# Attention with two feed-forward blocks on one Trainium2 core: how the last six result banks are evicted and stored

## The chip, the cores and the metric

The kernel runs on one NeuronCore of a Trainium2 chip. The metric is the device time of one execution in microseconds (us). The kernel before took 1049.45 us as the median of three runs (1048.07 to 1259.41).

## The reference

Everything is float32. Four batches of 576 rows and eight heads go through a thresholded softmax attention, and the result, as 2304 tokens of 512 numbers, through two feed-forward blocks:

```python
scores = scale * np.matmul(q, k.transpose(0, 1, 3, 2))
thresh = np.max(scores, axis=-1, keepdims=True) - tau
scores = np.where(scores >= thresh, scores, -1000000000.0)
...
h = x @ w_in
g = np.maximum(h, 0.0) + alpha * np.minimum(h, 0.0)
x = g @ w_out
...
a = x @ w1
b = x @ w2
h = a * b @ w3
return h @ w_out
```

The output is one array of 2304 rows of 512 float32 numbers (2 KB a row), batch after batch: rows 576 t to 576 t + 575 belong to batch t.

## The kernel before, in words

The kernel has three stages: attention, the first feed-forward block, and the second one. The change touches only how the second block's results leave the core.

**The second block.** w3 @ w_out is multiplied out beforehand (the tiles `wp`). The 2304 tokens are then taken in three passes (`NPASS`, L1181) of 768 tokens each, two halves of 384. In a pass the loop of L1381 goes over eight slices `f` of the hidden width. For each slice TensorE multiplies the moving tiles `T` by the stationary tiles `sw` in seven products (`product`, L1336, matmuls at L1341), ScalarE and VectorE put these together (`copy_of`, `tt`) and split the product into pairs `x`, and TensorE adds `x` times `wp` to six accumulating PSUM banks, `accs[0]` to `accs[5]` (`d_piece`, L1354, matmuls at L985). Four of these banks carry the name `acc`, two the name `h`. In the last slice of a pass each bank is finished by three matmuls, in the order 3, 4, 5, 0, 1, 2 (L1448).

**Evicting and storing.** When a bank is finished, `ev` (L1466) copies it to an SBUF tile `o` of 128 x 512, and `store` (L1469) sends that tile, 256 KB, to the output in DRAM from SyncE's queue. `GROUPS` (L1199) says which rows a bank holds. In passes 0 and 1, and in four banks of pass 2, these are 128 rows of one batch (every fourth of its first 512), which L1472 writes as 128 rows. Banks 4 and 5 of the last pass hold the last 64 rows of two batches each; L1475 addresses them as an array of 2 x 64 x 512, one transfer for both batches. So in the last pass the stores are, in order: one of 128 rows (bank 3), two of 2 x 64 rows (banks 4 and 5), and three of 128 rows (banks 0, 1, 2).

**What sets the order.** Each operation is given to a planner (`list_order`, L34) with the engines that may do it and an assumed cost. `{"A": 0.48, "V": 0.6}` at L1478 means ScalarE (A) or VectorE (V), whichever the planner finds earlier; "S" is SyncE, "T" TensorE, "D" a mark without an instruction. The planner's result is the order of the instructions on every engine; on the chip each engine then runs its own list in order and waits on semaphores where data is not there yet. In the kernel before the planner gave all eighteen evictions of L1467 to ScalarE.

After the last store, SyncE waits until all stores have landed (these waits have the line of the launch, L1517), and a few closing semaphores and drains end the program.

Of the kernel before, what the change touches and what calls it, by code (L numbers as in the profile page):

```python
# [120 lines left out]
def kernel(  # L121
# [25 lines left out]
    nc = tc.nc  # L147
    B, H, S, D = q.shape
# [8 lines left out]
    SM = 512  # L157
    ST = S - SM
# [62 lines left out]
    with tc.manual_schedule():  # L221
# [118 lines left out]
        for h in range(2):  # L340
# [4 lines left out]
            out=kscale, in0=tau_sb, scalar1=0.0, scalar2=1.0 / float(D) ** 0.5, op0=ALU.is_ge, op1=ALU.mult  # L345
# [223 lines left out]
        def op(key, P, engine, emit, deps=(), take=None, free=()):  # L569
            at = AT[key + "_0" if not P and key + "_0" in AT else key]  # L570
            ops.append(Op({engine: 0.0}, emit, PER * P + at, deps, take, free))
            named[key, P] = ops[-1]
            return ops[-1]
# [7 lines left out]
        for P in range(NPAIR):  # L581
            for n in "qk":
                ld = op("a" + n, P, "S", lambda e, P=P, n=n: load_pair(P, n), spl.get((P - 2, n), ()))
                spl[P, n] = []
                on = "P" if P else "V"
# [18 lines left out]
            for what in ("q", "tails", "k"):  # L604
# [7 lines left out]
                    take="ptp" if what == "tails" else "s",  # L612
# [3 lines left out]
                if what != "q":  # L616
# [7 lines left out]
                    free=[t],  # L624
# [4 lines left out]
            for what in ("q", "tails") if not P else ():  # L629
# [6 lines left out]
                    take="s" if what == "q" else "ptp",  # L636
# [7 lines left out]
                    free=[t],  # L644
# [5 lines left out]
            for j in range(9):  # L650
                u = 9 * P + j
                c, h = j // 2, j % 2
# [6 lines left out]
                    take="s",  # L659
# [11 lines left out]
                    take="praw" if j == 8 else "p" if h == 0 else None,  # L671
                    free=[Q, E],
# [12 lines left out]
                for g, src in groups:  # L685
# [7 lines left out]
                        take="ptp",  # L693
                        free=ms[:1],
# [7 lines left out]
                        take="pt" if new else None,  # L702
                        free=[T],
# [4 lines left out]
                if j in (3, 8):  # L708
                    half = int(j == 8)
                    V = op(  # L710
                        f"V{half}",
                        P,
                        "T",
                        lambda e, P=P, half=half: pv(P, half),
                        evd + [lv],
                        take="ptp",
                        free=[first],
                    )
# [8 lines left out]
                        free=[V],  # L727
# [3 lines left out]
        for f in range(NW):  # L731
            ld = op("w0", f, "S", lambda e, f=f: load_w_in(f), [w_done[f - 1]] if f else [])
            c = op("w1", f, "A", lambda e, f=f: low_w_in(f), [ld])
            m = [ld]
            for i in range(4):
# [6 lines left out]
                    take="m" if i == 0 else None,  # L742
# [4 lines left out]
            hi = op("w7", f, "A", lambda e, f=f: hi_w_in(e, f), [a])  # L747
# [289 lines left out]
        for t in order:  # L1037
# [4 lines left out]
            for f in range(NF):  # L1042
# [6 lines left out]
                    take="h",  # L1049
                    free=[hl[0] for hl in xl],  # L1050
# [20 lines left out]
                g = op({"V": part(n, 0.61)}, prelu, now + 3.5, [u], free=[hj])  # L1071
                h, l = split(n, lambda gt=gt, n=n: gt()[:, 0:n], gs, now + 4.3, [g], "gs", free=[u])

                def x2_job(e, f=f, n=n, acc=acc, gs=gs):
# [17 lines left out]
                    take="acc" if f == 0 else None,  # L1092
                    free=[h],
# [43 lines left out]
        for i in range(NF2):  # L1137
# [20 lines left out]
            for part_ in range(2):  # L1158
# [5 lines left out]
                    take=None if part_ else "h",  # L1164
                    free=[w3_ops[part_].slot],
# [15 lines left out]
        NPASS = B * S // (2 * HT)  # L1181
# [199 lines left out]
        for i, (p, f) in enumerate(order2):  # L1381
            if i + 2 < len(order2):
                S_of[i + 2], S_made[i + 2] = stationary(order2[i + 2][1], now + FP - 3)
            end = i == len(order2) - 1
            T_next = None
            if f == NF2 - 1 and p + 1 < NPASS:
                T_next = moving(p + 1, now + 1.0, None)
            s, m = S_of.pop(i), T_of
            made = S_made.pop(i)
            t = {n: temp() for n in ("u", "v", "c11", "c12")}  # L1390

            def J(k, bank_, first, deps, prio, s=s, m=m):
                o = pe(
                    6 * MH, lambda e: product(bank_, s[k], m[k], first), prio,
                    deps + [o for o in s[k][1]] + [m[k][1], m[k][2]],
                )
                if f == NF2 - 1:
                    o.free.append(m[k][1])
                    m[k][1].left += 1
                return o  # L1400

            def tt(dst, x, y, how, cost, prio, deps, take=None, free=(), engines=None):
                return op(
                    engines or {"V": cost},
                    lambda e: ENG[e].tensor_tensor(out=dst(), in0=x(), in1=y(), op=how),  # L1405
                    prio, deps, take=take, free=free,
                )

            def copy_of(dst, src, prio, deps):
                return op({"A": part(HT, 0.62)}, lambda e: nc.scalar.copy(out=dst(), in_=src()), prio, deps, take="ct")  # L1410

            bx, by = (x_bank, y_bank) if i % 2 == 0 else (y_bank, x_bank)
            X, Y = (lambda b=bx: b()[:, 0:HT]), (lambda b=by: b()[:, 0:HT])
            P_ = 0.56
            q = now
            j1 = J(1, bx, True, x_free, q)
            c1 = copy_of(t["u"], X, q + 1.3, [j1])
            j6 = J(6, by, True, y_free, q + 1.04)
            u2 = tt(t["u"], Y, t["u"], ALU.add, P_, q + 2.3, [j6, c1])
            d_next(q + 2.1, 2)  # L1420
            j2 = J(2, bx, False, [c1], q + 3.5)
            c11 = copy_of(t["c11"], X, q + 4.6, [j2])
            j5 = J(5, by, True, [u2], q + 4.5)
            v5 = tt(t["v"], Y, t["u"], ALU.add, P_, q + 5.8, [j5, u2], take="ct")
            d_next(q + 5.5, 2)
            j7 = J(7, bx, True, [c11], q + 6.9)
            c22 = tt(t["v"], X, t["v"], ALU.add, P_, q + 8.0, [j7, v5])
            j3 = J(3, by, False, [v5], q + 8.0)
            c12 = tt(t["c12"], Y, t["u"], ALU.add, P_, q + 9.1, [j3, u2], take="ct")
            d_next(q + 9.0, 1 if not end else 0)  # L1430
            j4 = J(4, bx, False, [c22], q + 9.7)
            c21 = tt(t["u"], X, t["u"], ALU.add, P_, q + 10.8, [j4, c12])
            d_next(q + 10.7, 1 if not end else 99)
            x_free, y_free = [c12], [c21]
            for h, l in made:
                h.left += 1
            j2.free.append(made[0][0])
            j5.free.append(made[1][0])
            j4.free.append(made[3][0])
            j3.free.append(made[2][0])  # L1440
            ab1 = tt(t["c12"], t["c12"], t["v"], ALU.mult, 0.56, q + 9.7, [c12, c22], free=[v5])
            ab0 = tt(t["u"], t["c11"], t["u"], ALU.mult, 0.56, q + 11.4, [c21, c11], free=[c11])
            gs = [None, None]
            for half, src, made_, frees, at in ((1, "c12", ab1, c12, 10.3), (0, "u", ab0, c1, 12.0)):
                g_ = part_pair("x", bufs=4)
                h, l = split(HT, t[src], g_, q + at, [made_], "x", free=[frees], costs=(0.66, 0.73))
                gs[half] = (g_, h, l)
            for g in (3, 4, 5, 0, 1, 2):  # L1448
                half = g // 3

                def go(prio, g=g, half=half, gs=gs, p=p, f=f):
                    last = f == NF2 - 1
                    _, h, l = gs[half]
                    o = pe(
                        3 * MF, d_piece(g, gs, f, f == 0, last), prio,
                        [h, l, wp_ops[f]] + (evicted[g] if f == 0 else []),
                    )
                    if g % 3 == 2:
                        o.free.append(h)
                        h.left += 1  # L1460
                    if not last:
                        return
                    on = ("u", "gs", "m")[g % 3] if p == NPASS - 1 else ("u", "gs")[g % 2]
                    out_ = lazily(lambda: dn.tile([128, 512], F32, tag=on, name="o", bufs=3 if on == "m" else 2))

                    def ev(e):  # L1466
                        (nc.scalar.copy if e == "A" else nc.vector.tensor_copy)(out=out_(), in_=accs[g]())  # L1467

                    def store(e):  # L1469
                        t_, c = GROUPS[p][g]  # L1470
                        if t_ < B:
                            dst = out[t_ * S : t_ * S + SM, :].rearrange("(p c) d -> p c d", c=4)  # L1472
                            nc.sync.dma_start(out=dst[:, c, :], in_=out_())
                        else:
                            dst = out.rearrange("(b s) d -> b s d", b=B)[2 * c : 2 * c + 2, SM:S, :]  # L1475
                            nc.sync.dma_start(out=dst, in_=out_())

                    v = op({"A": 0.48, "V": 0.6}, ev, prio + 0.7, [o], take=on)  # L1478
                    evicted[g] = [v]
                    s_ = op({"S": 0.65}, store, prio + 1.2, [v])  # L1480
                    op({"D": 0.0}, lambda e: None, prio + 1.3, [s_], free=[v]).wait[s_] = 2.0

                queue.append(go)
            if T_next:
                T_of = T_next
            now += FP
# [35 lines left out]
```

## Time and profile before

| what | us |
|---|---|
| median of three runs | 1049.45 |
| lowest of the three | 1048.07 |
| the profiled execution, its own time | 1048.38 |
| the profiled execution, span from first to last instruction | 1046.6 |
| TensorE busy in the span | 1012.8 |

The profiled execution's own time is 1.8 us more than its span. In the rows, PE is TensorE, DVE VectorE, ACT ScalarE and SP SyncE; a "q" behind an engine's name is its sequencer, where DMAs are issued. Times are from the start of the span. The last pass of the second block ends near 1032 us, and the stores of its banks follow.

### The profile page before, as it was taken

How to read it: one execution, taken by the hardware profiler on the slowest of the kernel's cores; microseconds unless marked ns; L12 is line 12 of the kernel's file. 1: busy time of each engine (PE TensorE's matmuls, PEld its weight loads, DVE VectorE, ACT ScalarE, POOL GpSimd, SP SyncE). 2: the span in 40 equal slices, each digit the busy share in tenths (PEclk: the TensorE clock that was granted, in tenths of full speed). 3: DMA queues.
4: the chain of work that ended last, by engine and by line, in shares of the span. 5: the costliest groups of instructions: out<-in, count | busy, mean ns of one | idle time of the engine just before them, and what ended most of it. 6: DMA issues, size and time to landing. Idle time of an engine off the chain costs nothing.

```text
span 1046.6 us, 16928 instructions
## 1 busy us (share of the span) xinstructions
PE 1012.8 (97%) x5870; PEld 865.4 (83%) x5870; DVE 751.5 (72%) x1552; ACT 583.5 (56%) x1122; POOL 340.8 (33%) x469
## 2 busy tenths in 40 slices
PE   8999999999989999999999999999999999999994
PEld 6778777777858889988888888888899999999993
DVE  7999999999858787666765565648476686676651
ACT  5998989999856555554444344323233363364321
POOL 4888888888633331222211111104100000000000
PEclk9999999999999999999999999999999999999998
DMA  5353434434113333344414334412332232224201
GB/s 129 88 148 92 135 105 123 117 104 136 38 41 121 112 110 112 132 141 151 172 60 151 119 108 150 147 38 69 101 116 86 82 133 79 89 74 146 71 1 60
DMA packets 71385, 109.50 MB, mean 105 GB/s; under 512 B 14852, under 2 KB 43524, under 8 KB 71300
## 3 DMA queue, kind: packets, MB, share of 16 engines
q1 hardware_dynamic: 69092, 108.42, 33.1%
q8 instruction: 46, 0.75, 0.3%
q10 hardware_dynamic: 2208, 0.01, 0.1%
q14 instruction: 39, 0.32, 0.1%
HBM read 80.22 MB, written 18.35 MB: 94 GB/s over the span
## 4 chain that ended last, share of the span: by engine, by line
PE 87%; POOL 6%; DVE 2%; issue 2%; ACT 1%; DMA 1%; POOLq 0%; DVEq 0%; ACTq 0%
PE h L985 25%; PE acc L985 24%; PE h L1341 17%; PE pv_ps L518 8%; PE s_ps L402 5%; PE pt_ps L491 5%; POOL p L474 3%; PE tr L291 2%; POOL ks L181 1%; POOL qs L181 1%; PE zero L352 1%; PE h L858 1%; POOL praw L474 1%; DMA raw<-in_moe_w_dram 1%; DVE sm L426 0%
## 5 line engine op out<-in xcount | busy, mean ns | idle before, releaser
L985 PE MATMUL h<-x,wa 128*128 128x512 f32 (+1 forms) x960 | 212.3, 371 | 1.2 <-ACT x L183 1.1
L985 PE MATMUL acc<-gs,wu 128*128 128x512 f32 (+1 forms) x960 | 209.7, 368 | 0.4 <-DVE wu L829 0.4
L985 PEld LDWEIGHTS h<-x,wa 128*128 128x128 f32 x960 | 167.3, 189 | 32.5 <-ACT x L183 2.9
L985 PEld LDWEIGHTS acc<-gs,wu 128*128 128x128 f32 x960 | 168.2, 189 | 30.8 <-DVE wu L829 0.8
L1341 PE MATMUL h<-T,sw 128*128 128x384 f32 x1008 | 190.5, 335 | 0.0
L1341 PEld LDWEIGHTS h<-T,sw 128*128 128x128 f32 x1008 | 178.4, 188 | 8.4
L218 POOL TENSOR_TENSOR m<-m,raw 128x512 int32<-128x512 int32 x58 | 81.7, 1409 | 280.5 <-DVE m L213 200.2
L1405 DVE TENSOR_TENSOR ct<-h,ct 128x384 f32<-128x384 f32 x120 | 66.9, 557 | 91.6 <-PE h L1341 91.4
L426 DVE TENSOR_REDUCE sm<-s_ps 128x1 f32<-128x576 f32 x144 | 105.6, 751 | 12.7 <-PE s_ps L402 12.5
L437 ACT ACTIVATE e<-s_ps,sm 128x576 f32<-128x576 f32 x144 | 106.2, 765 | 7.6 <-DVE sm L426 4.7
L474 POOL TENSOR_SCALAR p<-p,sm 128x576 f32<-128x576 f32 x128 | 97.2, 767 | 26.6 <-DVE sm L467 17.6
L451 DVE SCALAR_TENSOR_TENSOR p<-s_ps,sm,e 128x576 f32<-128x576 f32 x128 | 102.6, 811 | 0.9 <-ACT e L437 0.9
L183 ACT CAST gs<-g 128x512 fp32r<-128x512 f32 (+1 forms) x80 | 46.2, 578 | 94.1 <-PE acc L985 75.6
L491 PE MATMUL pt_ps<-ident,p 128*128 128x128 f32 x576 | 86.0, 276 | 11.5 <-ACT pt L505 8.9
L188 DVE TENSOR_TENSOR gs<-g,gs 128x512 fp32r<-128x512 f32 (+1 forms) x80 | 61.2, 765 | 46.5 <-ACT gs L183 45.8
L1056 ACT ACTIVATE g<-h,sign_sb 128x512 f32<-128x512 f32 (+1 forms) x80 | 51.3, 643 | 69.5 <-PE h L985 61.9
L1061 DVE SCALAR_TENSOR_TENSOR g<-h,salpha_sb,g 128x512 f32<-128x512 f32 (+1 forms) x80 | 55.6, 695 | 47.9 <-ACT g L1056 47.9
L491 PEld LDWEIGHTS pt_ps<-ident,p 128*128 128x128 f32 x576 | 64.5, 140 | 26.7 <-POOL praw L474 10.3
L518 PE MATMUL pv_ps<-pt,vraw 128*64 128x256 f32 (+1 forms) x640 | 84.7, 411 | 0.4 <-ACT xT L531 0.2
L183 ACT CAST sw<-w 128x512 fp32r<-128x512 f32 (+1 forms) x96 | 54.0, 569 | 55.4 <-PE h L1341 53.6
L505 ACT COPY pt<-pt_ps 128x512 f32<-128x512 f32 x128 | 74.5, 597 | 15.1 <-PE pt_ps L491 14.1
L985 PE MATMUL acc<-wp,x 128*128 128x512 f32 x288 | 81.9, 394 | 0.0
(119 smaller groups left out, 1521.9 us busy)
## 6 DMA issues: line engine op xcount, KB each, us to landing
raw<-in_moe_w_dram SPq DMA_DIRECT2D x32, 512.0 KB, 3.7
raw<-in_moe_w_out_dram SPq DMA_DIRECT2D x24, 512.0 KB, 3.5
w<-w SPq DMA_DIRECT2D x48, 256.0 KB, 2.6
qU<-qT SPq DMA_DIRECT2D x30, 320.0 KB, 3.5
w<-w SPq DMA_DIRECT2D x24, 384.0 KB, 2.9
wraw<-in_moe_w_in_dram SPq DMA_DIRECT2D x14, 512.0 KB, 3.7
w<-m SPq DMA_DIRECT2D x24, 256.0 KB, 2.1
z<-w SPq DMA_DIRECT2D x24, 256.0 KB, 2.7
```

What stands on the lines that cost most here:

```text
L183: eng.copy(out=dst, in_=src)
L218: nc.gpsimd.tensor_tensor(out=mc[0], in0=mc[0], in1=mc[1], op=ALU.add)
L426: nc.vector.tensor_reduce(out=sm_of(u, 0), in_=st[u], axis=AX.XY, op=ALU.max, negate=True)
L437: nc.scalar.activation(out=es[u].rearrange("p (j s) -> p j s", j=2), in_=st[u], func=AF.Exp, bias=sm_of(u, 0))
L451: nc.vector.scalar_tensor_tensor(out=p_at(u).rearrange("p (j s) -> p j s", j=2), in0=st.pop(u), scalar=sm_of(u, 1), in1=es.pop(u).rearrang ...
L474: nc.gpsimd.tensor_scalar(out=out, in0=in_, scalar1=sm_of(u, 3), scalar2=1.0, op0=ALU.mult, op1=ALU.mult)
L491: nc.tensor.transpose(t[:, i, :], p[:, at + i * 128 : at + (i + 1) * 128], ident)
L505: nc.scalar.copy(out=pt[:, g, 0:4, to], in_=ps)
L518: nc.tensor.matmul(out=o[64 * hh : 64 * hh + 64, 0:n], lhsT=vr[:, hh, i, :], rhs=pt[:, 0 if i == 4 and not half else hh, i, :], start=(i = ...
L985: nc.tensor.matmul(out=out, lhsT=l, rhs=r, start=first and i == 0, stop=last and i == n - 1)
L1341: nc.tensor.matmul(out=bank_()[:, 0:HT], lhsT=w()[:, ap_, kc * 128 : kc * 128 + 128], rhs=x()[:, bp, kc * HT : kc * HT + HT], start=first ...
L1405: lambda e: ENG[e].tensor_tensor(out=dst(), in0=x(), in1=y(), op=how),
```

## The change

Three things change, all in the eviction of finished banks.

- In passes 0 and 1 all evictions are assigned to ScalarE, at an assumed cost of 0.6.
- In the last pass banks 4, 5 and 0 are evicted by VectorE, banks 3 and 1 by ScalarE, and bank 2 in halves: columns 0 to 255 by ScalarE, 256 to 511 by VectorE.
- Banks 4 and 5 of the last pass are stored by two transfers each, of 64 rows (128 KB): the first batch's from SyncE's queue, the second batch's from ScalarE's queue.

```diff
-                    def ev(e):
-                        (nc.scalar.copy if e == "A" else nc.vector.tensor_copy)(out=out_(), in_=accs[g]())
-
-                    def store(e):
+                    final = p == NPASS - 1
+
+                    def ev(e, lo=0, hi=512):
+                        copy = nc.scalar.copy if e == "A" else nc.vector.tensor_copy
+                        copy(out=out_()[:, lo:hi], in_=accs[g]()[:, lo:hi])
+
+                    def store(e, part):
                         t_, c = GROUPS[p][g]
+                        queue_ = nc.scalar if e == "A" else nc.sync
                         if t_ < B:
                             dst = out[t_ * S : t_ * S + SM, :].rearrange("(p c) d -> p c d", c=4)
-                            nc.sync.dma_start(out=dst[:, c, :], in_=out_())
+                            queue_.dma_start(out=dst[:, c, :], in_=out_())
                         else:
-                            dst = out.rearrange("(b s) d -> b s d", b=B)[2 * c : 2 * c + 2, SM:S, :]
-                            nc.sync.dma_start(out=dst, in_=out_())
-
-                    v = op({"A": 0.48, "V": 0.6}, ev, prio + 0.7, [o], take=on)
-                    evicted[g] = [v]
-                    s_ = op({"S": 0.65}, store, prio + 1.2, [v])
-                    op({"D": 0.0}, lambda e: None, prio + 1.3, [s_], free=[v]).wait[s_] = 2.0
+                            r0 = (2 * c + part) * S + SM
+                            queue_.dma_start(out=out[r0 : r0 + ST, :], in_=out_()[64 * part : 64 * part + 64])
+
+                    tail_rows = GROUPS[p][g][0] == B
+                    if final and g == 2:
+                        vs = [
+                            op({"A": 0.35}, lambda e: ev(e, 0, 256), prio + 0.7, [o], take=on),
+                        ]
+                        vs.append(op({"V": 0.45}, lambda e: ev(e, 256, 512), prio + 0.71, [o, vs[0]]))
+                        vs[1].wait[vs[0]] = -0.3
+                    else:
+                        vs = [op({"V": 0.69} if tail_rows or final and g == 0 else {"A": 0.6}, ev, prio + 0.7, [o], take=on)]
+                    evicted[g] = vs
+                    sts = [op({"S": 0.6}, lambda e: store(e, 0), prio + 1.2, vs)]
+                    if tail_rows:
+                        sts.append(op({"A": 0.5}, lambda e: store(e, 1), prio + 1.25, vs))
+                    done_ = op({"D": 0.0}, lambda e: None, prio + 1.3, sts, free=vs[:1])
+                    for s_ in sts:
+                        done_.wait[s_] = 2.0
```

At the end of the program ScalarE's list changes as follows; `acc_8573` is bank 3, `acc_8613` bank 0, `acc_8634` bank 1, `acc_8652` bank 2, and the two `h` are banks 4 and 5.

```order
-L1467 COPY o<-acc_8573 128x512
-L1467 COPY o<-h 128x512 x2
-L1467 COPY o<-acc_8613 128x512
-L1467 COPY o<-acc_8634 128x512
-L1467 COPY o<-acc_8652 128x512
+L1470 COPY o<-acc_8573 128x512
+L1480 DMA out_dram<-o 64x512 x2
+L1470 COPY o<-acc_8634 128x512
+L1470 COPY o<-acc_8652 128x256
```

Three copies leave ScalarE, the last becomes half as wide, and two DMA issues stand ahead of the copy of bank 1.

VectorE's list, which ended with two subtractions of L188, now ends with these copies; in brackets is the engine whose semaphore each waits for.

```order
L188 TENSOR_TENSOR x_10856<-ct_10789,x_10856 128x384 [waits Activation_49]
L1470 COPY o_10870<-h_8578 128x512 [waits PE_49]
L1470 COPY o_10876<-h_8605 128x512 [waits PE_49]
L1470 COPY o_10883<-acc0_8613 128x512 [waits PE_49]
L1470 COPY o_10893<-acc2_8652 128x256 [waits Activation_49]
```

The copy of the second half of bank 2 waits for ScalarE (Activation), whose last instruction is the copy of the first half.

SyncE's list at the end of the program keeps its length; four of its stores stay whole and two become 64 rows.

```order
-L1473 DMA out_dram<-o 128x512
-L1476 DMA out_dram<-o 2x64x512 x2
-L1473 DMA out_dram<-o 128x512 x3
+L1477 DMA out_dram<-o 128x512
+L1480 DMA out_dram<-o 64x512 x2
+L1477 DMA out_dram<-o 128x512 x3
```

In passes 0 and 1 one copy moves on ScalarE, at the same place of both; `acc_8634` is bank 1, `acc_8652` bank 2, and `sw` a stationary tile for a later slice.

```order
-L1467 COPY o<-acc_8634 128x512
-L183 CAST x<-ct 128x384
+L1470 COPY o<-acc_8634 128x512
+L183 CAST x<-ct 128x384
+L1470 COPY o<-acc_8652 128x512
 L183 CAST sw<-w_10080 128x512
-L1467 COPY o<-acc_8652 128x512
```

The copy of bank 2 now stands ahead of the cast of `sw` instead of behind it. TensorE's order is the same in both kernels.

## Rows read from the trace of the kernel before

**Rows 1.** The page, busy time of each engine over the span.

```profile
PE 1012.8 (97%) x5870; PEld 865.4 (83%) x5870; DVE 751.5 (72%) x1552; ACT 583.5 (56%) x1122; POOL 340.8 (33%) x469
```

**Rows 2.** The chain that ended last, 1026 to 1047 us: start, duration, what.

```profile
1030.32 2.05 PE acc L985 x9
...
1032.39 0.59 ACT o L1467
```

**Rows 3.** Timeline of ScalarE, 1028.9 to 1033 us: start us, us, engine, line, what.

```profile
1028.97 0.59 ACT L1467 COPY o<-acc 128x512 f32<-128x512 f32 x1 [0.51 <-PE acc L985]
1029.67 1.27 ACT L1467 COPY o<-h 128x512 f32<-128x512 f32 x2
1031.04 1.95 ACT L1467 COPY o<-acc 128x512 f32<-128x512 f32 x3
```

**Rows 4.** Timeline of SyncE's queue, 1029 us to the end.

```profile
1029.59 0.34 SPq L1473 DMA_DIRECT2D out_dram<-o  x1
1030.28 1.30 SPq L1476 DMA_DIRECT2D out_dram<-o  x2
1031.65 4.73 SPq L1473 DMA_DIRECT2D out_dram<-o  x3
```

**Rows 5.** Waits of SyncE, 1028 us to the end: us in total, times, longest.

```profile
SPq L1517 <- DMA out_dram<-o: 9.1, 1, 9.1
```

**Rows 6.** Stores of L1473, 1032.3 to 1046 us: issue ns min/median/max, starts; landing.

```profile
L1473 SPq DMA_DIRECT2D out_dram<-o x3: 462/637/3432, 1031.7 to 1035.7; - x3
...
DMA to landing us min/median/max: 9.7/9.8/12.6
```

**Rows 7.** DMA in 40 slices, 1032.3 to 1046 us: tenths of 16 engines busy, rate.

```profile
DMA  0110111114589999971111111111111111111000
GB/s 36 42 18 36 36 24 42 30 48 90 120 317 353 341 323 329 347 245 60 48 54 48 54 54 48 54 48 54 48 54 54 48 48 54 54 48 48 30 0 0
```

**Rows 8.** Stores of L1476 (2 x 64 rows), issue ns min/median/max.

```profile
L1476 SPq DMA_DIRECT2D out_dram<-o x2: 538/598/659, 1030.3 to 1031.1; - x2
```

**Rows 9.** Store of L1473, 1028.9 to 1029.6 us (bank 3 of the last pass), landing.

```profile
DMA to landing us min/median/max: 2.1/2.1/2.1
```

**Rows 10.** Stores of L1473 in passes 0 and 1 (840 to 1000 us).

```profile
L1473 SPq DMA_DIRECT2D out_dram<-o x12: 332/338/402, 847.4 to 948.2; - x12
...
DMA to landing us min/median/max: 2.0/2.4/4.2
```

**Rows 11.** Transfers of L376, each from 64 rows of 5 KB in SBUF to 64 others.

```profile
L376 SPq DMA_DIRECT2D qU<-qT x30: 483/560/1837, 21.2 to 272.9; - x30
...
DMA to landing us min/median/max: 3.4/3.5/4.9
```

**Rows 12.** DMA in 40 slices, 21 to 25.5 us, two transfers of L376 issued at 21.2.

```profile
DMA  0000000700009749644982995001996994699849
```

**Rows 13.** The first of two DMAs that ScalarE's queue issues before, issue ns min/median/max.

```profile
L224 ACTq DMA_DIRECT2D tau_sb<-in_tau_dram x1: 435/435/435, 0.7 to 0.7; - x1
```

**Rows 14.** Groups by shape: copies from PSUM: busy us, mean ns, idle before.

```profile
L863 DVE COPY y<-h 128x512 f32<-128x512 f32 x13 | 8.9, 686 | 4.8 <-PE h L858 4.4 <-issue 0.3
L1105 DVE COPY xT<-acc 128x256 f32<-128x256 f32 x1 | 0.4, 425 | 1.4 <-PE acc L985 1.4
...
L1105 ACT COPY xT<-acc 128x256 f32<-128x256 f32 x3 | 0.9, 382 | 0.4 <-PE acc L985 0.4
```

**Rows 15.** Timeline, 853.7 to 860 us: the last two banks of pass 0.

```profile
854.60 0.86 PE L985 MATMUL acc<-wp,x 128*128 128x512 f32 x3
...
854.79 0.62 ACT L183 CAST sw<-w 128x512 fp32r<-128x512 f32 x1
...
855.54 0.59 ACT L1467 COPY o<-acc 128x512 f32<-128x512 f32 x1
...
856.55 0.48 ACT L1410 COPY ct<-h 128x384 f32<-128x384 f32 x1 [0.43 <-PE h L1341]
...
857.66 0.56 DVE L1405 TENSOR_TENSOR ct<-h,ct 128x384 f32<-128x384 f32 x1 [0.78 <-PE h L1341]
```

## Prediction

> **What bounds the kernel now.** First the page's busy times: TensorE is busy for 97% of the span [rows 1]. Over nearly all of it nothing but less TensorE work would help, and the change takes none away and leaves TensorE's order alone. So only what comes after the last matmul can move the time, and I read that stretch row by row.
>
> The chain that ended last stops at the copy of the last bank, 1032.39 + 0.59 = 1032.98 us [rows 2]. The span ends at 1046.6. That leaves 13.6 us in which no engine computes: 1.3% of the time. SyncE's queue shows what fills it. The six stores should follow the six copies, which start 0.7 us apart [rows 3]. The first three do: issued at 1029.59, 1030.28 and about 1031.05 [rows 4]. The fourth starts to issue at 1031.65, and this issue alone takes 3.43 us [rows 6], where a store of the same shape takes 0.34 in passes 0 and 1 [rows 10]. So the sixth, whose data is there at 1032.98, begins only at 1035.7 and lands 9.7 to 9.8 us later, at about 1045.5 [rows 6]. SyncE waits 9.1 us for that landing [rows 5], and closing semaphores and drains take the rest, some 1.0 us.
>
> Why is landing so slow? From 1038.5 to 1045 the DMA view shows one tenth of the sixteen engines busy and about 53 GB/s, while in the seven slices before it all are busy and move 317 to 353 GB/s [rows 7]. One tenth of sixteen is about two engines, and 53 GB/s is about a sixth of the full rate. The two transfers that come just ahead of the held issue are those of 2 x 64 rows [rows 4, 8]; their outermost dimension has two entries. My reading: each runs on two engines only, and the same two. Their 512 KB at 53 GB/s need 9.9 us, and the two engines' shares of the next three stores (2/16 of 768 KB, 98 KB, 1.9 us) stand behind them, so these cannot land earlier either. Together with the first microseconds, where the rate is only about 36 GB/s [rows 7], that fills the time up to 1044.
>
> **The change part by part.**
>
> *The two split stores.* Out go two transfers of 2 x 64 rows; in come four of 64 rows. Do 64 rows spread over all engines? The trace shows no store of 64 rows, but it shows transfers of 64 rows, L376: in a stretch in which at first two of these alone run, the engines reach nine tenths busy [rows 12], and one of 320 KB lands in 3.5 us [rows 11]; on two engines at 53 GB/s it would need 6.2 us for the data alone. I take full spread. At some 335 GB/s [rows 7] a bank of 256 KB is then 0.78 us of work for the engines. The first bank landed 2.1 us behind its issue at 1029.59 [rows 4, 9], at 1031.7; five more at that rate make 1035.6 the earliest landing of the last.
>
> On this the Trainium skill has a rule, on its page "DMA: Bandwidth & Descriptors", section "Why a DMA increments its semaphore by 16 and not by 1": a transfer from SyncE's or ScalarE's queue uses the largest number of engines, up to 16, that divides the slowest dimension of both its sides. By that rule 2 x 64 rows get two engines, as rows 7 have it, and 64 rows sixteen, which no store here shows; the sum by the rule is the one above, and by the worst that the rows leave open it is the second rival's.
>
> *Issues.* A 64-row issue on SyncE takes 0.48 to 0.56 us, as with L376 [rows 11]; on ScalarE's queue the nearest row has 0.435 [rows 13]. As bounds I take 0.33 (the shortest store of passes 0 and 1 [rows 10]) and 3.43 (the held issue [rows 6]); my value is 0.44 to 0.56, from the nearest rows.
>
> *Three copies on VectorE.* A copy of 128 x 512 from PSUM takes 0.686 us there [rows 14], against 0.59 on ScalarE [rows 3], and TensorE delivers a bank each 0.68 to 0.7 us. VectorE can just follow: bank 4 from 1029.67 to 1030.36, bank 5 to 1031.05, bank 0 to 1031.75. That is 0.1 us later each than before, and nothing queues behind them on VectorE but the half of bank 2.
>
> *ScalarE's list.* Bank 3 until 1029.56; then the issue for bank 4's second half waits for VectorE until 1030.38 and takes until 1030.9; the issue for bank 5's waits until 1031.08 and takes until 1031.6. Only behind these stands the copy of bank 1, which TensorE delivers near 1031.7 (ScalarE took it up at 1031.7 before: the last of the three copies in the third of rows 3 begins at 1032.39, the one ahead of it 0.68 earlier). So the issues fit into the wait, with 0.1 us to spare; if each took 0.1 more, bank 1 would be late by that.
>
> *The halved bank.* Bank 2 is delivered at 1032.37 [rows 2]. ScalarE's half takes 0.38 us [rows 14]: 1032.39 to 1032.77. VectorE's half waits for ScalarE's by the order of the instructions, so the two halves run one after the other: 0.03 hop, then 0.425 [rows 14], done at 1033.23. Before, the whole copy was done at 1032.98. The halving costs 0.25 us instead of saving 0.2.
>
> *The last store.* It can be issued at 1033.26, since nothing holds SyncE's queue any more. Landing takes 2.0 to 4.2 us for the stores of passes 0 and 1, 2.4 in the median [rows 10], and 2.1 for the first one of the last pass [rows 9]. I take 2.4, since the transfers come about as fast as the engines move them: landed at 1035.7, just behind the 1035.6 that the rate allows. With the closing 1.0 us the span ends at 1036.7.
>
> *Passes 0 and 1.* The copy of bank 2 moves ahead of a cast of `sw`. Before, the cast ran from 854.79 to 855.41 and the copy from 855.54 to 856.13 [rows 15]. Now the copy waits for TensorE until the same 855.5, and the cast follows until 856.7, behind a wait that hid it. Queued behind it is the copy of `ct` (before at 856.55), late by about 0.2 us; what needs it, VectorE's addition at 857.66, waits for TensorE anyway [rows 15]. The price is nothing. Without that cover it would be 0.2 us in each of two passes.
>
> *The sum.* Last landing 1045.5 before, 1035.7 after: 9.8 us less. The span goes from 1046.6 to about 1036.7, and the execution from 1048.38, which is 0.1% below the median of 1049.45, to 1038.5. This is 0.95% off, and a measurement of this kernel can tell about 2% from no change, so my verdict is "within 2%" although I expect a real gain.
>
> **The rivals.**
>
> *ScalarE's queue holds its issues.* If an issue there takes as long as SyncE's held one, 3.43 us each, the copies behind it are late: issues until 1033.8 and 1037.3, bank 1 until 1037.9, the halves of bank 2 until 1038.3 and 1038.75, landing at 1041.2, span 1042.2, execution 1044.0. For it: that queue has issued only two small DMAs in this trace, both at the start. Against: the one in the rows took 0.44 us [rows 13], and SyncE's was held behind transfers that the change removes.
>
> *The 64-row pieces do not spread (the slow side).* Then 512 KB still go through two engines, with the old landing of 9.8 us behind the last issue, and now ScalarE stands in the same jam as SyncE did: its second issue is held 3.43 us from 1031.1 until 1034.5, bank 1 is copied until 1035.1, bank 2's halves until 1036.0, and the last store, issued at 1036.0 instead of 1035.7, lands 0.3 us later: 1048.7; with both issues held, the last store goes out at 1038.8 and the time is 1051.4. It decides as soon as a 64-row store gets at most two or three engines. Rows 11 and 12 speak against it.
>
> *The split gains nothing.* If the landing were slow for a reason that has to do with where these rows lie in DRAM and not with the number of engines, two pieces would take as long as one: 1048.4 and 0.25 for the halves, 1048.6. For it: the trace shows no store of 64 rows. Against: the share of two engines in rows 7. The page on DMA of the Trainium skill, "Rules for kernel authors", advises against this very change: two transfers to disjoint partition halves are not worth it, one of 128 partitions should be used, since both run on the same sixteen engines. That holds where the one transfer has sixteen; the rows before show it with two, so I give this rival little.
>
> **How the numbers follow.** Forecast as worked out: 0.80, time 1038.5, own range 1036.8 (landing of 2.0 instead of 2.4, the rest from the 1.4 us between the runs of 1048.07 and 1049.45) to 1040.5 (landing of 4.2). ScalarE's queue: 0.12, 1044.0. No spread: 0.05, 1048.7 to 1051.4. No gain: 0.03, 1048.6. The range of 1036.8 to 1044.0 leaves out the last two cases and some of the first. All cases lie between 1028.5 and 1070.4, the bounds of 2%: faster 0.01, same 0.97, slower 0.02, these for what none of the cases names.
>
> **What would show it.** Right: SyncE's issues all under 0.7 us, none of 3.4; no trickle at one tenth of the engines; the last landing near 1035.7 and SyncE's final wait about 2 us; in the chain ScalarE's and then VectorE's half of bank 2. Wrong: a landing of over 5 us for any store, an issue on ScalarE's queue of over 1 us and a late copy of bank 1, or an idle TensorE near 856 and 948.

## The result and the profile after

The changed kernel takes 1039.66 us in the median of four runs (1039.3 to 1122.32), the kernel before 1049.03 (four runs with the same lowest and highest time as above). The ratio is 0.9913, 95% interval 0.989 to 0.9935: 0.9% less time, which by the bound of 2% is "within 2%" and by the interval is a real gain. The forecast was 1038.5 us. The medians also hold runs that a disturbance slowed (1259.41 and 1122.32); the ratio leaves these out.

All of the gain lies behind the last matmul. The timeline of TensorE after the change, 1030.2 to 1034 us, ends with the same nine matmuls as in [rows 2], at 1032.67 instead of 1032.37 us:

```profile
1030.46 2.21 PE L985 MATMUL acc<-wp,x 128*128 128x512 f32 x9
```

From there the span of before runs on for 14.2 us (to 1046.6), that of after for 5.2 us (to 1037.9). The timeline of the copies and of the two queues after the change, 1027 us to the end, answers to [rows 3, 4]:

```profile
1029.27 0.59 ACT L1470 COPY o<-acc 128x512 f32<-128x512 f32 x1 [0.51 <-PE acc L985]
1029.88 0.34 SPq L1477 DMA_DIRECT2D out_dram<-o  x1
1029.96 1.39 DVE L1470 COPY o<-h 128x512 f32<-128x512 f32 x2 [0.61 <-PE h L985]
1030.68 1.19 SPq L1480 DMA_DIRECT2D out_dram<-o  x2
1030.69 1.44 ACTq L1480 DMA_DIRECT2D out_dram<-o  x2
1031.35 0.69 DVE L1470 COPY o<-acc 128x512 f32<-128x512 f32 x1
1032.07 1.86 SPq L1477 DMA_DIRECT2D out_dram<-o  x3
1032.17 0.91 ACT L1470 COPY o<-acc 128x512 f32<-128x512 f32 x2 [2.31 <-DVE o L1470]
1033.11 0.42 DVE L1470 COPY o<-acc 128x256 f32<-128x256 f32 x1 [1.07 <-ACT o L1470]
```

No issue is held any more: the three last stores take 1.86 us together on SyncE's queue, where they took 4.73 [rows 4]. The last row shows VectorE's half of bank 2 waiting for ScalarE's; it ends at 1033.53.

The last store of after (L1477 from 1033.5 us on: issue and landing) and SyncE's final wait answer to [rows 5, 6]:

```profile
L1477 SPq DMA_DIRECT2D out_dram<-o x1: 368/368/368, 1033.6 to 1033.6; - x1
...
DMA to landing us min/median/max: 3.3/3.3/3.3
```

```profile
SPq L1533 <- DMA out_dram<-o: 2.9, 1, 2.9
```

And the DMA view of after, 1030 to 1037.2 us in 40 slices, answers to [rows 7]: the long stretch at one tenth of the engines is gone.

```profile
DMA  0000999700599899979698999999899963100000
GB/s 0 0 0 0 387 398 387 285 0 0 148 216 182 216 421 387 387 262 262 193 296 273 262 285 330 376 421 398 330 398 410 398 228 137 46 23 0 0 0 0
```

The store is issued, as forecast, as soon as its data is there, but it lands 3.3 us later, not 2.4. In most of the slices in the middle the engines are busy at 150 to 300 GB/s, in others at about 400. What that is, the experiments below show.

### The profile page after: what moved, and what is told of

Its sections match the earlier page's. It is cut to its first block, busy times and chain, and to the rows that moved or that the text cites. A ratio compares the mean times of both kernels' runs of the same rounds, so it can differ in the third digit from the quotient of the medians.

```text
span 1037.9 us, 16931 instructions
## 1 busy us (share of the span) xinstructions
PE 1014.1 (98%) x5870; PEld 867.0 (84%) x5870; DVE 751.6 (72%) x1556; ACT 580.6 (56%) x1119; POOL 340.1 (33%) x469
## 4 chain that ended last, share of the span: by engine, by line
PE 87%; POOL 5%; issue 2%; DVE 2%; ACT 2%; DMA 1%; SPq 0%; POOLq 0%; ACTq 0%; DVEq 0%
PE h L985 25%; PE acc L985 24%; PE h L1341 17%; PE pv_ps L518 8%; PE pt_ps L491 5%; PE s_ps L402 5%; POOL p L474 3%; PE tr L291 2%; POOL ks L181 1%; POOL qs L181 1%; PE zero L352 1%; PE h L858 1%; DMA raw<-in_moe_w_dram 0%; POOL praw L474 0%; ACT qT L311 0%
## 5 line engine op out<-in xcount | busy, mean ns | idle before, releaser
L188 DVE TENSOR_TENSOR gs<-g,gs 128x512 fp32r<-128x512 f32 (+1 forms) x80 | 60.0, 750 | 47.0 <-ACT gs L183 46.4
```

## The experiments

The theory: a transfer of 2 x 64 rows runs on two engines, and the stores behind it wait for these two. The rivals: that VectorE's evictions or the second queue bring the gain; that it is not the number of engines but where the short transfers lie or how small they are. TensorE's last matmul ends between 1031.2 and 1033.7 us in the profiled executions of these kernels, whose matmuls do the same work, so I compare two things: the ratio to the kernel before, and the time from the last matmul's end to the span's end (the "tail"), taken from one trace of each kernel; how far tails differ between executions of one kernel is not shown. Each ratio goes by runs of the kernel before that were taken beside that kernel: 1049.03 us in the median for the change, 1047.84 to 1048.14 for the others.

| kernel | median us | ratio to before (95%) | tail us |
|---|---|---|---|
| before | 1049.03 | 1 | 14.2 |
| changed | 1039.66 | 0.9913 (0.989 to 0.9935) | 5.2 |
| split alone | 1039.07 | 0.9916 (0.9902 to 0.9929) | 5.4 |
| evictions alone | 1047.99 | 1.0 (0.9991 to 1.0009) | 14.2 |
| 62 rows | 1047.32 | 0.9992 (0.9983 to 1.0001) | 13.6 |
| 61 rows | 1057.35 | 1.0089 (1.0076 to 1.0103) | 23.1 |
| bank 2 whole | 1040.15 | 0.992 (0.9905 to 0.9935) | 5.2 |
| one queue | 1039.24 | 0.9913 (0.9899 to 0.9928) | 5.4 |
| rows interleaved | 1037.5 | 0.9896 (0.988 to 0.9913) | 4.0 |
| every second partition | 1038.82 | 0.9913 (0.99 to 0.9927) | 5.2 |

**The split alone.** The kernel before with this edit:

```diff
-                            dst = out.rearrange("(b s) d -> b s d", b=B)[2 * c : 2 * c + 2, SM:S, :]
-                            nc.sync.dma_start(out=dst, in_=out_())
+                            for part in range(2):
+                                r0 = (2 * c + part) * S + SM
+                                nc.sync.dma_start(out=out[r0 : r0 + ST, :], in_=out_()[64 * part : 64 * part + 64])
```

> The kernel before with one edit: banks 4 and 5 of the last pass go out as two transfers of 64 rows each, all from SyncE's queue; every eviction stays whole and on ScalarE. Theory 1 (the time was lost because a transfer of 2 x 64 rows runs on two engines): the whole gain is here, 1039.7 us within 0.7, no issue over 0.7 us, no tail at one tenth of the engines. Rival (the gain needs VectorE's evictions or the second queue, because four issues of 0.5 us on one queue hold the later stores): the last store is issued 1 us or more later than with all three edits and the time is 1040.7 or more.

Measured 1039.07 us, ratio 0.9916: the whole gain. SyncE's queue, 1027 us to the end:

```profile
1030.92 0.34 SPq L1473 DMA_DIRECT2D out_dram<-o  x1
1031.62 2.44 SPq L1477 DMA_DIRECT2D out_dram<-o  x4
1034.15 1.52 SPq L1473 DMA_DIRECT2D out_dram<-o  x3
```

Four issues of some 0.6 us do hold the later stores, as the rival said, though by 0.7 us and not by 1 or more: the last store goes out 1.6 us behind the last matmul (1033.71), against 0.9 us with all three edits. Yet the tail is longer by only 0.2 us, since this store then lands in 2.7 us instead of 3.3. The rival had a delay right and its price wrong.

**The evictions alone.** The changed kernel with the single transfer put back:

```diff
-                            r0 = (2 * c + part) * S + SM
-                            queue_.dma_start(out=out[r0 : r0 + ST, :], in_=out_()[64 * part : 64 * part + 64])
+                            dst = out.rearrange("(b s) d -> b s d", b=B)[2 * c : 2 * c + 2, SM:S, :]
+                            queue_.dma_start(out=dst, in_=out_())
...
-                    if tail_rows:
-                        sts.append(op({"A": 0.5}, lambda e: store(e, 1), prio + 1.25, vs))
```

> The changed kernel with the single transfers of 2 x 64 rows put back: VectorE's evictions and the halved bank alone. Theory 1: no gain at all, the held issue of about 3.4 us and the tail at one tenth of the engines are back, 1048.6 us (0.25 us worse than before for the halves run one after the other). Rival (the evictions on two engines bring part of the gain): 1046 us or less.

Measured 1047.99 us, ratio 1.0. The three last stores and SyncE's final wait (two views):

```profile
L1477 SPq DMA_DIRECT2D out_dram<-o x3: 462/670/3416, 1031.2 to 1035.3; - x3
...
DMA to landing us min/median/max: 9.7/9.8/12.6
```

```profile
SPq L1531 <- DMA out_dram<-o: 9.0, 1, 9.0
```

These are the rows of before [rows 5, 6] again. The 0.25 us for the halves does not show either, and the ratio's interval of 0.9 us to either side could not tell it; the rows say why it need not show: the last store is issued at 1035.3 us, long after the copies, behind the held issue.

**62 and 61 rows.** The changed kernel, with n = 62 and with n = 61:

```diff
-                            queue_.dma_start(out=out[r0 : r0 + ST, :], in_=out_()[64 * part : 64 * part + 64])
+                            queue_.dma_start(out=out[r0 : r0 + n, :], in_=out_()[64 * part : 64 * part + n])
```

> The changed kernel with 62 rows in each of the four short stores instead of 64; it leaves out the last 2 rows of each batch (8 of 2304). Theory 1 in the form that the number of engines is the largest divisor up to 16 of the rows: 62 gives two engines, 508 KB at 53 GB/s are 9.6 us, so the tail is back and the time 1047 to 1051 us. Rival (the short transfers are fast because they are contiguous in DRAM or small): 1039.5 us, as with 64 rows.

> The same with 61 rows; it leaves out the last 3 rows of each batch (12 of 2304). Theory 1: 61 is a prime, so one engine, 500 KB at 26.5 GB/s are 18.9 us and the three later stores' shares 1.9 us more: 1054 to 1060 us. Rival: 1039.5 us; a rival in which any count that is no multiple of 16 falls back to two engines: the same as with 62 rows.

Measured 1047.32 and 1057.35 us. Two rows fewer of 64 take nearly all of the gain away (the ratio's interval reaches 1), and one row fewer still costs 10 us more: neither the size nor the place in DRAM changes enough for that, the count of engines does. The rule that the forecast took from the Trainium skill ("DMA: Bandwidth & Descriptors", "Why a DMA increments its semaphore by 16 and not by 1": the largest divisor up to 16) now has three points here: 64 rows with all engines, 62 with two, 61 with one. The DMA view with 62 rows (1032.3 to 1046 us) and with 61 rows (1032.3 to 1055.6 us):

```profile
GB/s 90 167 239 203 203 173 155 221 317 287 275 185 96 66 48 54 54 48 48 54 54 48 54 48 54 48 54 54 48 48 54 54 48 42 12 0 0 0 0 0
```

```profile
GB/s 4 21 25 25 28 25 25 28 25 257 302 236 134 42 25 155 257 77 39 25 25 25 28 25 25 25 28 25 25 28 25 25 25 28 25 25 25 14 0 0
```

The trickle is about 51 GB/s with 62 rows, as before, and 26 with 61: one engine moves some 26 GB/s. The traces count the engines in a second way. Beside the 2 KB packets of data there are small ones; the DMA views of the last stores, first before (1025 to 1047 us), then after the change (1030 to 1037.9 us), give their number:

```profile
DMA packets 836, 1.57 MB, mean 72 GB/s; under 512 B 68, under 2 KB 68, under 8 KB 836
```

```profile
DMA packets 896, 1.57 MB, mean 199 GB/s; under 512 B 128, under 2 KB 128, under 8 KB 896
```

With 62 rows the same view counts 72 small packets, with 61 rows 68. All four come out as 16 for each whole store and each store of 64 rows, two for each of 2 x 64 rows or of 62 rows, and one for each of 61 rows: 68 is 4 x 16 + 2 x 2, 128 is 8 x 16, 72 is 4 x 16 + 4 x 2, and 68 again 4 x 16 + 4 x 1. One small packet from each engine that serves a store would give just that.

The three last stores with 62 rows also part two things that the forecast had told together:

```profile
L1477 SPq DMA_DIRECT2D out_dram<-o x3: 355/363/1268, 1031.4 to 1032.9; - x3
...
DMA to landing us min/median/max: 11.6/11.8/11.9
```

Here no issue is held for 3.4 us; the last store begins to issue at 1032.9, as soon as its data is there, and needs 1.27 us for it. It still lands only 11.6 us after that start. So the held issue in the kernel before is a symptom, not the cause. What sets the end is the work that waits on the two engines, and a store issued earlier only waits longer there.

**Bank 2 whole, and one queue.** Two single edits to the changed kernel; the first evicts bank 2 by ScalarE alone, the second issues all four short stores from SyncE:

```diff
-                    if final and g == 2:
+                    if False:
```

```diff
-                    sts = [op({"S": 0.6}, lambda e: store(e, 0), prio + 1.2, vs)]
-                    if tail_rows:
-                        sts.append(op({"A": 0.5}, lambda e: store(e, 1), prio + 1.25, vs))
+                    parts = (0, 1) if tail_rows else (0,)
+                    sts = [op({"S": 0.6}, lambda e: [store(e, i) for i in parts], prio + 1.2, vs)]
```

> The changed kernel with bank 2 of the last pass evicted whole by ScalarE instead of in halves by ScalarE and VectorE. If the last copy's end sets the last landing, the store goes out 0.25 us earlier and the time falls by 0.25 us to 1039.4. Rival (the DMA engines are the bound of the last 5 us, and the last store waits its turn behind the earlier ones): the store goes out 0.25 us earlier, lands at the same time, and the time stays at 1039.7.

> The changed kernel with all four stores of 64 rows issued from SyncE's queue, none from ScalarE's. Theory (the second queue only shares out issue time, and the queue that is left has time enough): ScalarE copies bank 1 up to 0.2 us earlier, SyncE's last issue is at most 0.3 us later, 1039.7 us within 0.4. Rival (two transfers from two queues run beside each other on the engines, two from one queue one after the other at half the rate, since each reads only 64 of the 128 partitions): the last landing is 0.7 us or more later, 1040.4 or more.

Measured 1040.15 and 1039.24 us, ratios 0.992 and 0.9913: neither can be told from the changed kernel. With bank 2 whole, the last store is issued 0.65 us behind the last matmul instead of 0.9, and lands in 3.4 us instead of 3.3: the rival (the engines bound the end) has the tail right, 5.2 and 5.2. The times alone could not tell the expected 0.25 us. With one queue the tail is 5.4, so the second queue is worth at most 0.2 us here, and the rival's 0.7 us or more is out.

**Rows interleaved.** If the engines bound the end at 200 to 300 GB/s, why not at 400? Every short store reads only one half of the 128 partitions. The kernel before with this edit lays row s of both batches side by side, so that one transfer of 64 x 2 rows reads all partitions:

```diff
-                copy(out=xT[B][:, pr, b * ST : (b + 1) * ST], in_=o[:, 256 : 256 + ST])
+                pair = xT[B][:, pr, 128 * (b // 2) : 128 * (b // 2) + 128].rearrange("p (s i) -> p i s", i=2)
+                copy(out=pair[:, b % 2, :], in_=o[:, 256 : 256 + ST])
...
-                            dst = out.rearrange("(b s) d -> b s d", b=B)[2 * c : 2 * c + 2, SM:S, :]
+                            dst = out.rearrange("(b s) d -> s b d", b=B)[SM:S, 2 * c : 2 * c + 2, :]
```

> The kernel before with one other edit: the 64 last rows of two batches are laid into a bank in turn (row s of both batches side by side) instead of one batch after the other, so that a bank goes out by one transfer of 64 x 2 rows with 64 as its outermost size; all evictions whole and on ScalarE. Theory 1: all sixteen engines serve it, and as no transfer reads only half of the partitions, the last store lands 2.1 to 2.5 us behind its issue at about 1033.3 instead of 3.3: 1038.2 to 1038.9 us, faster than both kernels. Rival (the engines' rate is the same for transfers of 64 and 128 partitions and bounds the end): 1039.4 to 1039.7. If it is the size of 2 anywhere in the shape that matters: 1048.4.

Measured 1037.5 us, the fastest of all, ratio 0.9896. The last matmul and copy of its chain, its three last stores, and its DMA view from 1030 to 1036 us:

```profile
1030.51 2.06 PE acc L986 x9
...
1032.59 0.59 ACT o L1468
```

```profile
L1474 SPq DMA_DIRECT2D out_dram<-o x3: 332/393/573, 1031.8 to 1033.2; - x3
...
DMA to landing us min/median/max: 2.4/2.6/2.7
```

```profile
DMA  0000899940029999999999999999999999000000
GB/s 0 0 0 0 328 423 423 423 151 0 0 96 382 410 369 410 342 410 355 423 383 437 423 410 369 396 355 369 437 396 423 423 369 355 0 0 0 0 0 0
```

Once the second bank starts, the engines run at some 340 to 440 GB/s without a dip, and the tail is 4.0 us, 1.2 less than with the change (the intervals of the two ratios overlap; the tails do not depend on the other stages). The 1.2 us have two parts: the last store is issued 0.6 us behind the last matmul instead of 0.9, and it lands in 2.4 us instead of 3.3. A transfer with 64 as its outermost size uses all engines, whether a 2 stands behind it or not; a 2 in front is what cost the time.

**Every second partition.** To tell "64 rows" from "half of the partitions", the interleaved kernel with two short stores a bank, each reading every second partition:

```diff
-                            dst = out.rearrange("(b s) d -> s b d", b=B)[SM:S, 2 * c : 2 * c + 2, :]
-                            nc.sync.dma_start(out=dst, in_=out_())
+                            for i in range(2):
+                                r0 = (2 * c + i) * S + SM
+                                nc.sync.dma_start(out=out[r0 : r0 + ST, :], in_=out_()[i::2])
```

> The interleaved kernel with each of its two transfers of 64 x 2 rows replaced by two of 64 rows on SyncE's queue, each reading every second of all 128 partitions (the kernel with the split alone reads the lower 64 partitions, then the upper 64, at about 210 GB/s, with the engines busy and a 2 KB packet taking 153 ns instead of 84). Theory (the rate is halved because only half of the partitions are read at a time): here the transfers of 64 rows run at the full rate where the issues let them, and the end lies 4.1 to 4.6 us behind the last matmul (against 5.4 with the split alone and 4.1 interleaved), limited by the 0.6 us of each issue. Rival (it is the 64 rows, four to an engine, whatever partitions they come from): the rate stays near 210 GB/s and the end 5.2 us or more behind the last matmul.

The DMA view of four microseconds in which the short stores run, first of this kernel (1029 to 1033 us), then of the split alone (1031.5 to 1035.5 us):

```profile
DMA  0028999995000499600289930069950039982499
GB/s 0 0 102 328 369 389 471 410 369 185 0 0 0 184 389 471 246 21 0 102 328 389 389 103 0 0 246 471 389 185 21 0 143 369 430 307 62 164 389 471
```

```profile
DMA  0038999993000796995879929679499289996969
GB/s 0 0 143 328 389 492 389 369 389 123 0 0 20 205 287 143 246 205 143 205 184 266 287 61 266 164 205 307 102 246 287 62 205 266 205 246 143 225 184 349
```

Behind the first store (whole, the first run of nines in both) each short store that reads every second partition is a burst at about 400 GB/s and then a pause until the next issue; where it reads 64 neighbouring ones, the engines are busy as long as the issues are apart, at about 200 GB/s. So the rival (64 rows as such) is out. The theory holds in a narrower form: both kinds of store read 64 of the 128 partitions, and the rate depends on which 64. The trace after the change fits this: from 1032.5 to 1033 us each of the two queues has a short store under way, one from the lower half and one from the upper, and the engines move 393 GB/s. The expected tail of 4.1 to 4.6 us was wrong all the same: it is 5.2, and the time, 1038.82, is no better than with the change. Four issues of 0.594 us follow one another on one queue, and the last store goes out as late as with the split alone.

## Why the prediction was right, point by point

- **What bounds the end.** Two engines serve a transfer of 2 x 64 rows: shown by the split alone (all of the gain), the evictions alone (none), the dose of 62 and 61 rows and the count of small packets. One reading was off without effect: the slices of [rows 7] at 317 to 353 GB/s are six, not seven. The forecast's story was one step too simple in naming the held issue beside the landing: with 62 rows the issue is not held, and the end is almost the same.
- **Spread of 64 rows.** Taken as full from the L376 rows; right. The slow side, in which they do not spread, is out.
- **Issues.** 0.44 to 0.56 us forecast. SyncE's were 0.50 and 0.52, ScalarE's 0.56 and 0.75. The rival of a held ScalarE queue is out; bank 1's copy began some 0.15 us late, and bank 2, which waits for TensorE anyway, took that up.
- **Copies.** VectorE's 0.69 us each kept pace. The halves ran one after the other and ended 0.86 us behind the last matmul (1033.53 against 1032.67), as worked out (1033.23 against 1032.37); whole on ScalarE it was 0.61 before. The expected 0.25 us of loss, however, costs nothing: with bank 2 whole the tail is the same. The forecast's other way to the landing, the time that the engines need for the banks, was the one that bounds.
- **The last landing.** This is the term that was off: 2.4 us from issue to landing, measured 3.3 (and SyncE's final wait 2.9 us, not about 2). I had the engines move the last five banks at 335 GB/s without a pause. In the split alone the short stores move at 202 GB/s (1033 to 1035.2 us); in the changed kernel, where at times two of them run together, the engines move 273 GB/s from 1031.8 to 1034.4 us, against 386 in the interleaved kernel (1031.7 to 1035.1 us), whose last store lands in the 2.4 us of the forecast. That the lower rate makes up the whole 0.9 us is worked out from these rates; no run changes the rate alone. The 0.9 us, and TensorE's end 0.3 us later in this execution, is the 1.2 us between the forecast span of 1036.7 and 1037.9.
- **Passes 0 and 1.** Forecast at nothing. In the timeline after (853.5 to 860 us) the cast of `sw` now follows the copy, and `ct`, which the forecast had 0.2 us late, and VectorE's addition keep their places to TensorE's rows, all 0.3 us later than in [rows 15]:

```profile
854.90 0.86 PE L985 MATMUL acc<-wp,x 128*128 128x512 f32 x3
...
855.84 0.59 ACT L1470 COPY o<-acc 128x512 f32<-128x512 f32 x1 [0.76 <-ACT x L183]
...
856.32 0.62 ACT L183 CAST sw<-w 128x512 fp32r<-128x512 f32 x1
...
856.86 0.48 ACT L1410 COPY ct<-h 128x384 f32<-128x384 f32 x1
...
857.97 0.56 DVE L1405 TENSOR_TENSOR ct<-h,ct 128x384 f32<-128x384 f32 x1 [0.78 <-PE h L1341]
```

- **The advice against two transfers of half the partitions** (the Trainium skill, "DMA: Bandwidth & Descriptors", "Rules for kernel authors") was set aside because the one transfer had two engines. That was right for the choice at hand; but the interleaved kernel, which does follow the advice with one transfer over all 128 partitions, has the shorter tail (4.0 us against 5.4 with the split alone).

## What to carry to other kernels

At the end of a kernel read the DMA view before the queues: engines at one tenth or less with a steady low rate meant here a transfer that ran on two or one of them, and every later store waited behind it, however early it was issued. Look at the outermost size of both sides of such a transfer, and put one there that 16 divides, as 64 here; where the data can be reordered so that one transfer over all partitions does it, that had the shorter tail than two halves. The copies made earlier were worth nothing here as long as the engines were behind.

## What was not expected of the hardware

A store that reads 64 neighbouring partitions moved at about 200 GB/s with the engines busy, one of the same 64 rows from every second of 128 partitions in bursts at about 400. And an issue of 64 rows takes longer than most of 128: 0.50 to 0.60 us on SyncE's queue against 0.34 to 0.44 after the change (the last store of 128 rows in the kernel with bank 2 whole took 0.61), while those of 62 rows took 0.24 and 0.32 us there and 0.26 and 0.52 on ScalarE's (the stores of L1480 with 62 rows, issue ns min/median/max):

```profile
L1480 SPq DMA_DIRECT2D out_dram<-o x2: 242/282/322, 1030.0 to 1030.7; - x2
L1480 ACTq DMA_DIRECT2D out_dram<-o x2: 256/386/517, 1030.0 to 1030.7; - x2
```

Why that is so was not tried.
